# Last layer of a fused attention, mixture and feed-forward kernel: reordering scalar work, preparation steps and row gathers around the block products

## The chip, the cores and the metric

The kernel runs on 1 core of one Trainium2 chip. The metric is the device time of one execution in microseconds (us). Engines are named PE (matrix products), DVE (vector), ACT (scalar), POOL (GpSimd) and SP (which issues most DMAs); each works through its own queue of instructions in program order. L1286 means line 1286 of the kernel before.

## The reference, cut to what matters

An attention with pooled keys and values feeds a top-2 mixture of 8 experts; its 4608 rows of 512 numbers feed the last layer, the only part that the change touches:

```python
def _moe2_ref(x, w_in, w_out):      # x: 4608 x 512, w_in: 512 x 2048, w_out: 2048 x 512
    h = x @ w_in
    g = h * np.cos(h)
    return (g @ w_out).astype(np.float32)
```

The rows of x are sums of two gated expert outputs, which lie in an HBM buffer `yb` in the experts' order and have to be gathered row by row.

## The kernel before

All products are made from pairs of 16-bit numbers, high and low part, with three matmuls for each product. The order of each engine's work is the order of the program; the kernel schedules by hand.

**Chunks and quarters.** The last layer is a loop over 9 chunks of 512 rows (`c`, 0 to 8), and in each over 4 quarters (`q_`) of the 2048 columns of h. A quarter makes four blocks of h (b = 0 to 3) by seven block products in Strassen's manner (`prod`, L1215, 12 matmuls of 256 columns each), in the order 1, 2, 6, 7, 5, 3, 4. Three PSUM tiles carry them: `pb` takes products 1, 6, 5, 3 in turn, each added to what is there, `pa` takes 2, `pc` takes 7 and then 4. Between the products stand the matmuls of the quarter before that multiply g with w_out (`down`, L1245; `some(n)` issues n groups of three).

**What ties PE to the other engines.** After product 1, 6 and 5 ACT copies `pb` into scratch (L1274, L1286, L1294), and the next product into `pb` has to wait for that copy. DVE adds `pa` or `pc` to the copies (L1282, L1295, L1303); product 4 has to wait until L1295 has read `pc`. 

**The activation of a block.** `act_a` takes two DVE operations (L1222, L1223: the reduction of the angle) and two ACT operations (L1224 sine, L1225 square). `act_b`, issued later, takes one DVE operation (L1233), one ACT operation (L1234, the high part of g) and one on POOL (L1235, the low part). Block 2's `act_b` is issued in the next quarter, behind L1274.

**Preparation of the next chunk.** While chunk c runs, steps made by `prepare(c + 1)` fetch and convert the next chunk's rows: `gather` (two indirect DMAs from POOL, L1024, into one of four `yg` buffers), `comb1a` (ACT, L1033, writes the single `x2` tile), `comb1b` (DVE, L1039 and L1040), `comb2a` and `comb2b` (the scale: small DVE operations and one transposition on PE, L110), `sub` (DVE, L1079), `opa` (ACT, L1087) and `opb` (DVE, L1091, then a DMA transposition from SP). `opa` writes one of two `x2h` buffers, or spare room of the current `ht` tile. The four row blocks of a chunk have i = 0 to 3; the seven operands of the products have o = 0 to 6. There are nine steps, two slots for them in a quarter: slot A behind L1274 and block 2's `act_b`, ahead of L1282, and slot B behind product 7 and block 0's `act_b`, ahead of L1294. Step 9 (`opa` and `opb` of operand 6) is left for the next chunk's first quarter.

Of the kernel before, what the change touches and what calls it, by code (L numbers as in the profile page):

```python
# [12 lines left out]
AF = mybir.ActivationFunctionType  # L13
# [21 lines left out]
def tile_attn_moe_ffn(ctx: ExitStack, tc: tile.TileContext, q, k, v, wgate, wnoise, noise,  # L35
                      w1, w2, win, wout, out):
    nc = tc.nc
    V, A, PL, PE, SP = nc.vector, nc.scalar, nc.gpsimd, nc.tensor, nc.sync
# [580 lines left out]
    for u in range(NU):  # L619
        g, r, n = UNITS[u]  # L620
# [106 lines left out]
    def psum(nm, bufs):  # L727
        return pp_.tile([128, 512], F32, name=nm, bufs=bufs)
# [288 lines left out]
    NCF = len(CHF)  # L1017
    X2, GT, CB = {}, {}, {}

    def gather(c, i):  # L1020
        g, r = CHF[c][i]
        yg = wp.tile([128, 2, 512], F32, name="yg", bufs=4)
        for kk in range(2):
            PL.indirect_dma_start(out=yg[:, kk, :], out_offset=None, in_=yb[0:512 * E * (c + 1), :] if c < 2 else yb[:, :],  # L1024
                                  in_offset=bass.IndirectOffsetOnAxis(ap=yidx[:, g, kk, r:r + 1], axis=0))
        CB["yg", c, i] = yg
# [77 lines left out]
    def prepare(c, room):  # L1104


        def many(*x):
            return lambda: [f(c, *a) for f, *a in x]

        return [many((gather, 0), (gather, 1)),  # L1110
                many((gather, 2), (gather, 3), (comb1a, 0), (comb1a, 1)),
                many((comb1b, 0), (comb1b, 1), (comb1a, 2), (comb1a, 3)),
                many((comb1b, 2), (comb1b, 3), (comb2a,)),
                many((comb2b,), (opa, 0), (opa, 1), (opa, 2, room)),
                many((opb, 0), (opb, 1), (opb, 2), (sub, 3)),
                many((sub, 4), (sub, 5), (opa, 3), (opa, 4), (opa, 5, room)),
                many((opb, 3), (opb, 4), (opb, 5), (sub, 6)),
                many((opa, 6), (opb, 6))]

# [3 lines left out]
    for j in range(NJ + 1):  # L1123
        up = [(mm1, j, f) for f in range(8)] if j < NJ else []
        dn = []
        if j > 0:
            e, c = JOBS[j - 1]
# [76 lines left out]
    UB, DN, GQ = {}, {}, {}  # L1204
    PRODS = {1: (0, 0), 2: (1, 1), 3: (6, 2), 4: (2, 6), 5: (3, 3), 6: (4, 5), 7: (5, 4)}

    def prod(c, q_, n, ps, start):
        a_, b_ = PRODS[n]
        x = xt_tile(c, b_).rearrange("p (i s k) n -> p i s k n", i=2, s=2)
        for h in range(2):  # L1210
            f = 128 * (2 * q_ + h)
            o = ps[:, 256 * h:256 * h + 256].rearrange("p (i n) -> p i n", i=2)
            for k_ in range(2):
                for j, (sa, sb) in enumerate(((0, 0), (0, 1), (1, 0))):
                    PE.matmul(o, FW["in"][4 * a_ + 2 * sa + k_][:, f:f + 128], x[:, :, sb, k_, :],  # L1215
                              start=(start and h == 0 and k_ == 0 and j == 0), stop=(k_ == 1 and j == 2), skip_group_check=True)

    def act_a(c, q_, b, h):

        k4 = CB["k4", c]  # L1220
        y = wp.tile([128, 512], F32, name="ty", bufs=4)
        V.tensor_scalar(y, h, k4[:, 0:1], k4[:, 0:1], op0=OP.add, op1=OP.subtract)  # L1222
        V.tensor_sub(y, h, y)  # L1223
        A.activation(y, y, AF.Sin, scale=k4[:, 1:2])  # L1224
        A.activation(y, y, AF.Square, scale=math.sqrt(2.0 * CC))  # L1225
        UB[b] = (c, q_, h, y)

    def act_b(b):
        if b not in UB:
            return  # L1230
        c, q_, h, y = UB.pop(b)
        g = GQ[c, q_]
        V.scalar_tensor_tensor(y, y, CC, h, op0=OP.subtract, op1=OP.mult)  # L1233
        A.activation(g[:, 2 * b, :], y, AF.Copy)  # L1234
        PL.tensor_sub(g[:, 2 * b + 1, :], y, g[:, 2 * b, :])  # L1235

    def down(c, q_, b, tt, h):

        def f():
            t = 2 * (b % 2) + tt  # L1240
            if (c, t) not in DN:
                DN[c, t] = psum("ph", 4)
            ps, g, k_ = DN[c, t], GQ[c, q_], 8 * (b // 2) + 2 * q_ + h
            for i, (a_, b_) in enumerate(((0, 0), (0, 1), (1, 0))):
                PE.matmul(ps, g[:, 2 * b + a_, 256 * h + 128 * tt:256 * h + 128 * tt + 128], FW["out"][b_][:, k_, :],  # L1245
                          start=(q_ == 0 and b < 2 and h == 0 and i == 0), stop=(q_ == 3 and b > 1 and h == 1 and i == 2))
            if q_ == 3 and b > 1 and h == 1:
                g, r = CHF[c][t]
                o_ = wp.tile([128, 512], F32, name=("yt", "tm")[t % 2], bufs=2)
                A.activation(o_, ps, AF.Copy, scale=CB["k4", c][:, 2:3])  # L1250
                SP.dma_start(dap(out, (1152 * g + r) * 512, [[9 * 512, 128], [1, 512]]), o_)
        return f

    load_wout[1]()
    ds, st = [], []

    def some(n):
        for f in ds[:n]:
            f()
        del ds[:n]  # L1260

    def step():
        if st:
            st.pop(0)()

    for c in range(NCF):
        for q_ in range(4):
            if q_ == 0 and c + 1 < NCF:
                st += prepare(c + 1, lambda: g[:, 14:16, :])
            g = GQ[c, q_] = wp.tile([128, 16, 512], F16, name="ht", bufs=2)  # L1270
            cw = g[:, 8:16, :].rearrange("p a n -> p (a n)").bitcast(F32).rearrange("p (a n) -> p a n", n=512)
            pb, pa, pc = psum("py", 2), psum("pt", 2), psum("py", 2)
            prod(c, q_, 1, pb, True)
            A.activation(cw[:, 0], pb, AF.Copy)  # L1274
            act_b(2)
            if q_ == 0 and c and st:
                step()
            if q_ == 0 and c + 1 < NCF or q_:
                step()
            some(2)  # L1280
            prod(c, q_, 2, pa, True)
            V.tensor_add(cw[:, 0], pa, cw[:, 0])  # L1282
            act_a(c, q_, 0, cw[:, 0])
            some(2)
            prod(c, q_, 6, pb, False)
            A.activation(cw[:, 1], pb, AF.Copy)  # L1286
            some(2)
            prod(c, q_, 7, pc, True)
            act_b(0)
            if len(st) > 1 or q_ < 3:  # L1290
                step()
            some(1)
            prod(c, q_, 5, pb, False)
            A.activation(cw[:, 2], pb, AF.Copy)  # L1294
            V.tensor_add(cw[:, 2], pc, cw[:, 2])  # L1295
            act_a(c, q_, 3, cw[:, 2])
            some(2)
            prod(c, q_, 3, pb, False)
            act_a(c, q_, 1, pb)
            act_b(3)  # L1300
            some(1)
            prod(c, q_, 4, pc, False)
            V.tensor_add(cw[:, 1], pc, cw[:, 1])  # L1303
            act_b(1)
            act_a(c, q_, 2, cw[:, 1])
            some(16)
            ds += [down(c, q_, b, tt, h) for b in (0, 1, 3, 2) for tt in range(2) for h in range(2)]
    act_b(2)
# [29 lines left out]
```

## Time and profile before

| what | value |
|---|---|
| time, median of 3 runs | 1908.68 us (1900.23 to 1909.55) |
| profiled execution, own time | 1910.69 us |
| its span | 1908.9 us, 29354 instructions |
| PE busy over the span | 1737.7 us (91%) |
| DVE, ACT, POOL busy | 63%, 43%, 22% |
| last layer (first block product to the end) | from 1155.85 us on |

The page counts a matmul as busy from its issue to a modelled end, so neighbouring matmuls overlap. The rows below are read as: start, duration, engine, line, operation, tiles written and read, shape, count; in brackets how long the engine sat idle before it and for whom it waited. Times run from the start of the span.

### The profile page before, as it was taken

To read this page: it belongs to the slowest core of one execution; us is meant where nothing else is said; L and a number is where in the kernel's file an instruction comes from. 1 tells how busy PE (TensorE), PEld (TensorE's weight loads), DVE (VectorE), ACT (ScalarE), POOL (GpSimd) and SP (SyncE) were. 2 spreads that over 40 slices of the span, in tenths; PEclk is the share of its full clock that TensorE was granted. 3 is DMA by queue.
4 is the path that set the end of the run, shared out by engine and by line. 5 is a ranking of instruction groups with operands and counts; after the bars stand their busy time and mean duration, and the time that the engine had idled before them with its cause. 6 is when DMAs were issued, how large, how long until landed. Compare 5 with 4: busy or idle time off the path is not lost.

```text
span 1908.9 us, 29354 instructions
## 1 busy us (share of the span) xinstructions
PE 1737.7 (91%) x11657; PEld 1024.6 (54%) x11657; DVE 1203.0 (63%) x2190; ACT 825.2 (43%) x1602; POOL 420.3 (22%) x456
## 2 busy tenths in 40 slices
PE   5877755599999999999999997999999999999999
PEld 3555433246444644464445544666666666666665
DVE  6786465463657466535775143877878787787864
ACT  3655434133233333232333233555555555555554
POOL 1225534100000000000110012243242323424221
PEclk7988867699999999999999998999999999999999
DMA  9977323447553654555653543122231312213100
GB/s 264 314 242 288 133 78 144 122 162 206 141 182 97 192 159 151 194 139 157 185 177 86 210 138 116 34 73 57 66 75 32 88 34 72 74 49 89 34 29 23
DMA packets 233212, 243.56 MB, mean 128 GB/s; under 512 B 154352, under 2 KB 167664, under 8 KB 232432
## 3 DMA queue, kind: packets, MB, share of 16 engines
q1 hardware_dynamic: 210544, 183.97, 33.2%
q0 software_dynamic: 11520, 37.76, 6.0%
q10 hardware_dynamic: 11008, 19.93, 3.0%
q8 instruction: 92, 1.51, 0.3%
q14 instruction: 48, 0.39, 0.1%
HBM read 127.06 MB, written 78.12 MB: 107 GB/s over the span
## 4 chain that ended last, share of the span: by engine, by line
PE 43%; DVE 20%; ACT 11%; issue 4%; DMA 2%; ACTq 0%; DVEq 0%; POOL 0%; POOLq 0%; SPq 0%
PE ph L795 19%; PE py L820 18%; DVE ty L1223 5%; ACT ty L1224 5%; DVE ty L1222 4%; ACT ty L1225 4%; PE ph L1245 2%; DVE ty L1233 2%; PE py L1215 2%; DMA yg<-yb,yidx 2%; DVE ht L1091 1%; DVE ht L1282 1%; DVE x2h L1091 1%; PE py L835 1%; DVE x L1039 1%
## 5 line engine op out<-in xcount | busy, mean ns | idle before, releaser
L795 PE MATMUL ph<-xt,w 128*128 128x512 f16 (+1 forms) x2304 | 410.4, 336 | 9.6 <-DMA xt<-xs 9.6
L1245 PE MATMUL ph<-w,ht 128*128 128x512 f16 x1728 | 413.2, 379 | 0.0
L820 PE MATMUL py<-w,ht 128*128 128x512 f16 x1728 | 384.4, 379 | 0.2 <-DVE ht L808 0.2
L795 PEld LDWEIGHTS <-w 128*128 128x128 f16 x2304 | 214.8, 98 | 196.0 <-issue 14.6
L1235 POOL TENSOR_TENSOR ht<-ty,ht 128x512 f16<-128x512 f32 x144 | 181.4, 1271 | 469.6 <-ACT ht L1234 393.0
L808 DVE SCALAR_TENSOR_TENSOR ht<-ph,ht 128x512 f16<-128x512 f32 (+2 forms) x192 | 110.0, 574 | 269.3 <-ACT ht L807 269.2
L820 PEld LDWEIGHTS <-ht 128*128 128x128 f16 x1728 | 168.8, 98 | 199.0 <-DVE ht L808 0.7
L1245 PEld LDWEIGHTS <-ht 128*128 128x128 f16 x1728 | 169.2, 98 | 151.9 <-issue 0.3
L1215 PEld LDWEIGHTS <-st 128*128 128x128 f16 x1872 | 184.0, 98 | 93.1 <-issue 45.5
L1224 ACT ACTIVATE ty<-ty,k 128x512 f32<-128x512 f32 x144 | 103.9, 722 | 262.4 <-DVE ty L1223 248.1
L807 ACT ACTIVATE ht<-ph 128x512 f16<-128x512 f32 (+2 forms) x192 | 96.2, 502 | 182.5 <-PE ph L795 156.5
L1215 PE MATMUL py<-xt,st 128*128 128x256 f16 x1040 | 142.4, 276 | 23.7 <-ACT ht L1294 12.0
L823 ACT ACTIVATE yt<-py,ysc 128x512 f32<-128x512 f32 x72 | 49.3, 685 | 231.6 <-PE py L820 231.6
L1233 DVE SCALAR_TENSOR_TENSOR ty<-ty,ht 128x512 f32<-128x512 f32 x108 | 74.8, 692 | 110.8 <-ACT ty L1225 108.9
L1215 PEld LDWEIGHTS <-w 128*128 128x128 f16 x1152 | 113.2, 98 | 36.8 <-issue 1.0
L1215 PE MATMUL py<-w,st 128*128 128x256 f16 x832 | 111.7, 272 | 9.9 <-ACT ht L1286 6.4
L435 PE MATMUL xp<-vbd,et 128*64 128x144 f32 (+3 forms) x864 | 91.2, 354 | 22.1 <-issue 5.9
L1024 POOL DMA_INDIRECT yg<-yb,yidx x72 | 73.5, 1020 | 162.7 <-DMA yb<-yt 93.5
L1223 DVE TENSOR_TENSOR ty<-ht,ty 128x512 f32<-128x512 f32 x108 | 105.0, 972 | 3.7
L886 POOL TENSOR_TENSOR tm<-yg 128x512 f32<-128x512 f32 x32 | 34.4, 1076 | 302.2 <-DVE x L896 151.1
L1234 ACT ACTIVATE ht<-ty 128x512 f16<-128x512 f32 x144 | 90.1, 626 | 24.6 <-DVE ty L1233 24.6
L1222 DVE TENSOR_SCALAR ty<-ht,k 128x512 f32<-128x512 f32 x108 | 91.1, 844 | 8.0 <-DVE ht L1282 0.5
(240 smaller groups left out, 2084.5 us busy)
## 6 DMA issues: line engine op xcount, KB each, us to landing
yb<-yt ACTq DMA_DIRECT2D x72, 256.0 KB
st<-in_moe_w_dram SPq DMA_DIRECT2D x8, 2048.0 KB
yg<-in_moe_w_in_dram SPq DMA_DIRECT2D x32, 512.0 KB
yg<-in_moe_w_out_dram SPq DMA_DIRECT2D x32, 512.0 KB
yb<-zt SPq DMA_DIRECT2D x18, 768.0 KB
st<-in_moe_w_dram SPq DMA_DIRECT2D x8, 1536.0 KB
w<-in_k_dram SPq DMA_DIRECT2D x16, 512.0 KB
w<-in_v_dram SPq DMA_DIRECT2D x16, 512.0 KB
```

What stands on the lines that cost most here:

```text
L435: PE.matmul(xp[64 * b:64 * b + 64, c0:c0 + n], lhs[:, 64 * b:64 * b + 64], rhs, start=(c == cs[0][0]), stop=(c == cs[-1][0]), skip_group_c ...
L795: PE.matmul(ps[:, 0:n], w[:, a_, k_, 128 * f:128 * f + 128], xt[:, 4 * b_ + k_, 0:n], start=(i == 0), stop=(i == 11))
L807: A.activation(t[:, 0], p, AF.Relu)
L808: V.scalar_tensor_tensor(t[:, 1], p, 0.0, t[:, 0], op0=OP.max, op1=OP.subtract)
L820: PE.matmul(ps[0:m], ht[:, a_, f, 128 * t:128 * t + m], w[:, b_, f, :], start=(i == 0), stop=(i == 23))
L1215: PE.matmul(o, FW["in"][4 * a_ + 2 * sa + k_][:, f:f + 128], x[:, :, sb, k_, :], start=(start and h == 0 and k_ == 0 and j == 0), stop=(k_ ...
L1222: V.tensor_scalar(y, h, k4[:, 0:1], k4[:, 0:1], op0=OP.add, op1=OP.subtract)
L1223: V.tensor_sub(y, h, y)
L1224: A.activation(y, y, AF.Sin, scale=k4[:, 1:2])
L1233: V.scalar_tensor_tensor(y, y, CC, h, op0=OP.subtract, op1=OP.mult)
L1235: PL.tensor_sub(g[:, 2 * b + 1, :], y, g[:, 2 * b, :])
L1245: PE.matmul(ps, g[:, 2 * b + a_, 256 * h + 128 * tt:256 * h + 128 * tt + 128], FW["out"][b_][:, k_, :], start=(q_ == 0 and b < 2 and h == ...
```

## The change

It has three parts. (1) `act_a` is cut in two: the DVE pair stays, the ACT pair (sine, square) becomes `act_s`, and for block 0 it is issued behind the copy L1286; for blocks 3, 1 and 2 it directly follows `act_a` as before. (2) Slot A moves from ahead of L1282 to behind block 0's `act_a`; what is left of the last chunk's steps (`own`) goes just ahead of it. (3) The gathers of a chunk move out of its own steps into the steps of the chunk before (quarters 2 and 3); a list of eight steps of its own serves chunk 1.

```diff
+        def rows(c, *i):
+            return [(lambda c_, i=i: gather(c, i), i) for i in i] if c < NCF else []
+        if c == 1:
+            return [many(*rows(1, 0, 1)),
+                    many(*rows(1, 2, 3)),
+                    many((comb1a, 0), (comb1a, 1)),
+                    many((comb1b, 0), (comb1b, 1), (comb1a, 2), (comb1a, 3)),
+                    many((comb1b, 2), (comb1b, 3), (comb2a,)),
+                    many((comb2b,), (opa, 0), (opa, 1), (opa, 2, room)),
+                    many((opb, 0), (opb, 1), (opb, 2), (sub, 3), (sub, 4), (sub, 5), (opa, 3), (opa, 4), (opa, 5, room),
+                         *rows(2, 0, 1)),
+                    many((opb, 3), (opb, 4), (opb, 5), (sub, 6), (opa, 6), (opb, 6), *rows(2, 2, 3))]
-        return [many((gather, 0), (gather, 1)),
-                many((gather, 2), (gather, 3), (comb1a, 0), (comb1a, 1)),
+        return [many((comb1a, 0), (comb1a, 1)),
                 many((comb1b, 0), (comb1b, 1), (comb1a, 2), (comb1a, 3)),
                 many((comb1b, 2), (comb1b, 3), (comb2a,)),
-                many((comb2b,), (opa, 0), (opa, 1), (opa, 2, room)),
+                many((comb2b,)),
+                many((opa, 0), (opa, 1), (opa, 2, room), *rows(c + 1, 0, 1)),
                 many((opb, 0), (opb, 1), (opb, 2), (sub, 3)),
-                many((sub, 4), (sub, 5), (opa, 3), (opa, 4), (opa, 5, room)),
+                many((sub, 4), (sub, 5), (opa, 3), (opa, 4), (opa, 5, room), *rows(c + 1, 2, 3)),
                 many((opb, 3), (opb, 4), (opb, 5), (sub, 6)),
                 many((opa, 6), (opb, 6))]
...
-        A.activation(y, y, AF.Sin, scale=k4[:, 1:2])
+        UB[b] = (c, q_, h, y)
+
+    def act_s(b):
+        c, _, _, y = UB[b]
+        A.activation(y, y, AF.Sin, scale=CB["k4", c][:, 1:2])
         A.activation(y, y, AF.Square, scale=math.sqrt(2.0 * CC))
-        UB[b] = (c, q_, h, y)
...
-            if q_ == 0 and c + 1 < NCF:
-                st += prepare(c + 1, lambda: g[:, 14:16, :])
+            if q_ == 0:
+                own, st = st, prepare(c + 1, lambda: g[:, 14:16, :]) if c + 1 < NCF else []
...
             act_b(2)
-            if q_ == 0 and c and st:
-                step()
-            if q_ == 0 and c + 1 < NCF or q_:
-                step()
             some(2)
             prod(c, q_, 2, pa, True)
             V.tensor_add(cw[:, 0], pa, cw[:, 0])
             act_a(c, q_, 0, cw[:, 0])
+            while own:
+                own.pop(0)()
+            step()
             some(2)
             prod(c, q_, 6, pb, False)
             A.activation(cw[:, 1], pb, AF.Copy)
+            act_s(0)
             some(2)
             prod(c, q_, 7, pc, True)
             act_b(0)
-            if len(st) > 1 or q_ < 3:
+            if c == 0 or len(st) > 1:
                 step()
...
             act_a(c, q_, 3, cw[:, 2])
+            act_s(3)
...
             act_a(c, q_, 1, pb)
+            act_s(1)
...
             act_a(c, q_, 2, cw[:, 1])
+            act_s(2)
```

## Rows read from the trace of the kernel before

**Rows 1.** Waits of PE in the last layer: us in total, times, longest.

```profile
PE py L1215 <- ACT ht L1286: 17.7, 25, 3.0
PE py L1215 <- ACT ht L1294: 15.3, 8, 8.5
```

**Rows 2.** Timeline of PE, chunk 0, quarter 3: product 1, product 4, next quarter.

```profile
1222.51 1.47 PE L1215 MATMUL py<-xt,w 128*128 128x256 f16 x12
...
1236.84 0.38 PE L1215 MATMUL py<-xt,w 128*128 128x256 f16 x2
...
1242.04 1.47 PE L1215 MATMUL py<-w,w 128*128 128x256 f16 x12
```

**Rows 3.** Timeline of PE, chunk 4: product 1, product 3; product 1 of the next two quarters.

```profile
1570.56 1.47 PE L1215 MATMUL py<-w,w 128*128 128x256 f16 x12
...
1585.07 1.47 PE L1215 MATMUL py<-w,st 128*128 128x256 f16 x12 [0.68 <-ACT ht L1294]
...
1592.22 1.47 PE L1215 MATMUL py<-w,w 128*128 128x256 f16 x12
...
1612.46 1.47 PE L1215 MATMUL py<-w,w 128*128 128x256 f16 x12
```

**Rows 4.** Timeline of PE, chunk 5: product 1 of quarters 2 and 3, then chunk 6.

```profile
1693.79 1.47 PE L1215 MATMUL py<-xt,w 128*128 128x256 f16 x12
...
1713.80 1.47 PE L1215 MATMUL py<-xt,w 128*128 128x256 f16 x12
...
1733.56 1.47 PE L1215 MATMUL py<-w,w 128*128 128x256 f16 x12
```

**Rows 5.** Timeline of ACT, chunk 4, quarter 0: sine, two copies, `comb1a`.

```profile
1579.71 0.72 ACT L1224 ACTIVATE ty<-ty,k 128x512 f32<-128x512 f32 x1 [3.25 <-DVE ty L1223]
...
1581.00 0.58 ACT L1286 ACTIVATE ht<-py 128x512 f32<-128x512 f32 x1
...
1582.39 0.71 ACT L1033 ACTIVATE x<-yg,gates 128x512 f32<-128x512 f32 x1
...
1584.44 0.58 ACT L1294 ACTIVATE ht<-py 128x512 f32<-128x512 f32 x1
```

**Rows 6.** Timeline of DVE, chunk 4, quarter 0 (three rows) and quarter 1 (two).

```profile
1574.49 0.69 DVE L1233 SCALAR_TENSOR_TENSOR ty<-ty,ht 128x512 f32<-128x512 f32 x1 [1.51 <-ACT ty L1225]
1576.49 1.13 DVE L1091 SCALAR_TENSOR_TENSOR x2h<-x,xt4s,x2h 128x512 f16<-128x512 f32 x1 [1.31 <-ACT x2h L1087]
...
1578.92 0.69 DVE L1223 TENSOR_TENSOR ty<-ht,ty 128x512 f32<-128x512 f32 x1
...
1602.81 0.74 DVE L1039 SCALAR_TENSOR_TENSOR x<-yg,gates,x 128x512 f32<-128x512 f32 x1
...
1606.34 0.23 DVE L104 COPY mbc<-xm 128x128 f32<-128x128 f32 x1
```

**Rows 7.** Timeline of DVE, chunk 5: block 2's second operation, then quarter 3.

```profile
1714.70 1.52 DVE L1223 TENSOR_TENSOR ty<-ht,ty 128x512 f32<-128x512 f32 x1
...
1723.30 0.69 DVE L1233 SCALAR_TENSOR_TENSOR ty<-ty,ht 128x512 f32<-128x512 f32 x1 [1.51 <-ACT ty L1225]
...
1727.41 0.68 DVE L1295 TENSOR_TENSOR ht<-py,ht 128x512 f32<-128x512 f32 x1
```

**Rows 8.** Timeline of POOL, same stretch: low parts of blocks 3 and 1.

```profile
1713.23 2.45 POOL L1235 TENSOR_TENSOR ht<-ty,ht 128x512 f16<-128x512 f32 x2 [6.65 <-ACT ht L1234]
```

**Rows 9.** Timeline of all engines, chunk 0, quarter 0 and the start of quarter 1.

```profile
1162.91 0.63 ACT L1234 ACTIVATE ht<-ty 128x512 f16<-128x512 f32 x1 [0.27 <-DVE ty L1233]
...
1172.70 2.72 PE L1215 MATMUL py<-xt,st 128*128 128x256 f16 x12 [8.54 <-ACT ht L1294]
...
1175.08 0.95 POOL L1024 DMA_INDIRECT yg<-yb,yidx  x1 [0.30 <-issue]
...
1178.64 1.47 PE L1215 MATMUL py<-xt,w 128*128 128x256 f16 x12 [0.78 <-DVE ht L1303]
```

**Rows 10.** Engine busy time by window; last columns: granted PE clock, DMA share, GB/s.

```profile
1160.00:1180.00 20.00, 9.23 (x61) 6.82 (x59) 7.53 (x12) 8.24 (x13) 9.85 (x10) 0.74 0.53 172
```

More of the change, by code (lines that the diff above doesn't have):

```diff
@@ L1264, in step @@
             st.pop(0)()
+    own = []
     for c in range(NCF):
         for q_ in range(4):
-            if q_ == 0 and c + 1 < NCF:
-                st += prepare(c + 1, lambda: g[:, 14:16, :])
+            if q_ == 0:
+                own, st = st, prepare(c + 1, lambda: g[:, 14:16, :]) if c + 1 < NCF else []
             g = GQ[c, q_] = wp.tile([128, 16, 512], F16, name="ht", bufs=2)
```

## The prediction

> **What bounds the kernel now.** I read the page first: the last layer is the stretch where PE is nearly always busy, and the change touches only that. Then the waits of PE there: almost all of its idle time is two waits, for the copy L1286 (25 times) and for the copy L1294 (8 times, once per chunk that prepares another), 33.0 us together [rows 1]. That is the prize. Then the timelines, quarter by quarter. A quarter without any wait takes 1242.04 - 1222.51 = 19.53 us [rows 2]; this is the floor, set by PE's own matmuls, and product 4 starts 14.33 into it. A common chunk loses against it: quarter 0 1592.22 - 1570.56 = 21.66, loss 2.13; quarter 1 20.24, loss 0.71 [rows 3]; quarter 2 20.01, loss 0.48 (of which 0.1 is the scale's transposition, which stays); quarter 3 19.76, loss 0.23 [rows 4]. Sum 3.55 us. The reader is to see that three of four quarters are already close to the floor, that quarter 0 holds most, and that each loss is an ACT or DVE instruction being late by less than a microsecond or two. So the question is where each late instruction stands after the change.
>
> **The sine pair behind L1286.** In quarter 0 L1286 starts only when the pair has ended: sine at 1579.71, L1286 at 1581.00 [rows 5], though its product had ended long before. Behind the change L1286 no longer waits for this pair, but slot A's ACT work now stands directly ahead of L1286, and slot A's DVE work stands behind L1223 of block 0.
>
> **Quarter 0, chunks 2 to 7.** Slot A now holds the left-over `opa`/`opb` of operand 6 and two `comb1a`. `comb1a` writes the single `x2` tile that `opb` still reads, so ACT waits for `opb`, which waits behind L1282, L1222 and L1223. In chunk 4's times: block 2's L1233 ends at 1575.18; from the end of `opb` (1577.62) to the end of L1223 (1579.61) the three operations take 2.0 [rows 6], so they now end at 1577.2. `opb` costs at most its 1.13: 1578.3. Two `comb1a` of about 0.7 [rows 5]: L1286 at 1579.7, 1.3 sooner than 1581.00, and product 5 is no longer late. But then the pair follows: L1286 0.55, from the sine to where slot B's `comb1a` starts 1582.39 - 1579.71 = 2.68, two `comb1a` 1.4: L1294 at 1584.3, against 1584.44 [rows 5]. Product 3 waits for it as before, and the wait, once split between two copies, now stands in one place. Loss 2.1 (bounds 1.8 to 2.8), where it was 2.13. The gather's landing no longer delays `comb1a`, but in the earlier chain that was worth only 0.7, which L1286 ahead of the pair takes back.
>
> **Quarter 1.** `comb1b` 2, 3 and `comb2a` now stand in slot A and `comb2b` in slot B of the same quarter. From the first of these L1039 to the end of the copy L104 it is 1606.57 - 1602.81 = 3.76 [rows 6]. They start when L1223 of block 0 ends, about 6.2 into the quarter (product 2 starts 2.6 in, 1.6 more to L1282, 2.0 for the three operations), so the copy is there at 9.9; PE reaches the transposition behind product 7 at about 9.5 and now waits 0.3 to 0.5, plus some 0.15 for each restart. A wait for L1274 of 0.2 to 0.7 comes on top, since quarter 0 hands on its lateness with three output copies in ACT's queue. Loss 1.2 (0.8 to 1.8), where it was 0.71.
>
> **Quarter 2.** Three `opa` on ACT fit ahead of L1286, the two gathers lie on POOL ahead of block 0's L1235, which nobody needs before the next quarter. Loss 0, where it was 0.48.
>
> **Quarter 3.** The third `opa` needs `sub` 5, which now comes behind L1223 of block 0: L1286 at 8.1 to 8.9 into the quarter, still in time for product 5. But the pair follows it, so L1233 of block 0 comes at 10.1 to 10.8; before it came at 1723.30 - 1713.80 = 9.50 and three `opb` and a `sub` put L1295 at 13.61, ending 14.3 [rows 4, 7]: just in time for product 4 (14.33 [rows 2]). Now L1295 ends at 14.9 to 15.7 and product 4 is late. Loss 0.8 (0.3 to 1.6), where it was 0.23.
>
> Sum of a common chunk: 2.1 + 1.2 + 0 + 0.8 = 4.1 (2.9 to 6.2) against 3.55. Six chunks: +3.3 us (-3.9 to +15.9).
>
> **DVE beside POOL.** L1223 takes 1.52 when POOL's L1235 runs beside it (1713.23 for 2.45), and 0.69 alone [rows 6 to 8]. Block 2's L1235 will now run while L1222 and L1223 of block 0 do, in quarters 0 and 3 above all, where up to now an `opb` or a `sub` lay beside it. That is up to 0.83 for each of these quarters, and it is what the upper bounds above hold; I take about a third: by the sums above L1222 and the low part become ready almost together, and where DVE comes first nothing in these rows says that it is slowed. The Trainium skill (SBUF — State Buffer, section "SBUF: two separate sides") says that the pair of ports which DVE and GpSimd share is locked for a whole instruction, and that the loser blocks. These rows agree with that; by the rule in its full force (0.55 more in two quarters of six chunks) the sum of six chunks would stand near +10 instead of +3.3.
>
> **Chunk 0.** In quarter 0 ACT waited for the first gathers, and with it L1294 and product 3 (8.54 idle, to 1172.70). After the change nothing stands between L1234 of block 0 (1162.91) and L1294: product 3 at 1164.1, 8.6 sooner. Its 12 matmuls ran in 2.72 instead of 1.47, at a granted clock of 0.74 over the stretch after that idle time [rows 9, 10]; at full clock quarter 1 starts some 1.0 sooner still: gain 9.6. Against that, POOL's gathers end no sooner (1176.03), and both low parts of blocks 3 and 1 (2.45 [rows 8]) stand behind them: 1178.5. PE, 9.6 earlier, wants block 1's low part at 1176.3 and waits 2.3. Quarters 1 and 2 lasted 1222.51 - 1178.64 = 43.87, 4.8 over the floor [rows 2, 9]; I count 2.3 there, 0.4 for block 0's low part, and 1.6 for `comb2b` followed at once by three `opa` ahead of L1294: 4.4 in all. Quarter 3 had no loss; now its slot A holds three `opb`, three `sub` and three `opa` in sequence and slot B three `opb`, a `sub`, `opa` 6, `opb` 6. L1286 comes behind the third `opa`, at 11.7, where product 5, due some 9.8 into the quarter, wants it begun by 9.1: 2.5; L1294 behind `opa` 6, which waits for `sub` 6 behind three `opb`: 4.1. With restarts 6.9. Chunk 0: 9.6 + 0.4 - 6.9 = 3.1 gained, less what a lowered clock after these waits costs: 0 to 6 (1.25 for each 12 matmuls at the lower level [rows 9]), taken as 2.5. So -0.6 (-3.1 to +3).
>
> **Chunks 1 and 8.** Chunk 1 has no left-over, so quarter 0's 2.13 go: -1.5 with the other quarters' changes. Chunk 8 has nothing to prepare: its wait for L1286 goes, 2.13 less the 0.84 for L1294: -1.3.
>
> **Sum:** +3.3 - 0.6 - 1.5 - 1.3 = -0.1 us. The profiled execution took 1910.69 (span 1908.9 and 1.8 around it), 2.0 above the median of the runs shown. So I predict 1910, the same within what can be told (0.5% of the time, 9.5 us).
>
> **Rivals.**
> 1. *The waits go and none comes back (faster).* If `comb1a` waits less for `opb`, L1295 in quarter 3 stays under 14.3 and the transposition finds its copy, seven preparing chunks win up to 3.4 each, 24 us, with chunk 8 and chunk 0's 3.1: 1882. For it: L1286 really leaves the pair's shadow, 17.7 us of waiting [rows 1], and DVE has slack behind L1223. Against it: the single `x2` tile, and a DVE queue that ended only just in time [rows 7]. If half of that comes true, 1896. Chance 0.25, between 1880 and 1900.
> 2. *The slowed pair and the long steps decide (slower).* L1223 of block 0 takes 1.52 in quarters 0 and 3, each chunk loses the upper 6.2: +15.9, chunk 0 +3, less 2.8: 1926. It decides from about 0.7 more in each of both quarters (six times 1.4 and 3.3 make over 9.5). For it: [rows 7, 8]; against it: it needs the low part to start first nearly every time. Chance 0.20, between 1920 and 1930.
> 3. *The change does not do what it says.* L1286 stays late because the steps' ACT work stands ahead of it, and the wait merely moves to L1294 and L1295. This is the forecast; 0.55, own range 1900 to 1919.
>
> **How the numbers follow.** The likeliest case is 3: 1910. Leaving out the far half of rival 1 and the far half of rival 2 (0.2 together) gives 1892 to 1923. Faster 0.25, same 0.55, slower 0.20.
>
> **What would show each step.** In the new trace: waits of PE for L1286 gone in chunks 1 to 8; waits for L1294 in quarter 0 of chunks 2 to 7 of about 2 us each; a wait of PE's L110 for L104; product 4 waiting for L1295 in quarter 3; in chunk 0 product 3 at 1164, a `down` group waiting for L1235 near 1178, and some 7 us of waits in quarter 3. The prediction is wrong if quarter 0 of the common chunks drops under 20.5 us (then rival 1) or quarter 3 rises over 21 (then rival 2).

## The result, and the profile after

The changed kernel takes 1927.88 us (median of 4 runs, 1925.05 to 1930.07); the kernel before takes 1909.12 beside it. The ratio on record is 1.0113, 95% interval 1.0086 to 1.014: 1.1% slower, above the predicted range of 1892 to 1923. (The ratios here and below are those on record; the quotient of the two medians can differ by some tenths of a per cent, 1.0098 here.) The profiled execution took 1926.75, with a span of 1925.0.

One warning before the spans are read. The last layer starts at 1155.85 in the profile of before and at 1147.69 in that of after; over the profiles of this study it lies between 1146.5 and 1162.8, though no kernel differs in the work ahead of it. So the measure used below is the *layer*: from the start of the first block product to the end of the span. Before it lasts 1908.90 - 1155.85 = 753.05, after 1925.0 - 1147.69 = 777.3: 24.3 longer.

Line numbers move: the block products L1215 are now L1228; L1286, L1294 and L1295 (copy of product 5, copy and sum of product 3 and 4) are L1302, L1311 and L1312; L1282 is L1295; L1274, the copy of product 1, is L1291; L1222, L1223 are L1235, L1236; L1233, L1234, L1235 are L1249, L1250, L1251; the output copy is L1266. L104, L110, L1024, L1033, L1039, L1087, L1091, L1092 keep theirs.

The waits of PE in the last layer, which answer to [rows 1] (us in total, times, longest):

```profile
PE pt L110 <- DVE mbc L104: 13.6, 8, 1.9
PE py L1228 <- ACT ht L1311: 13.1, 9, 1.7
PE py L1228 <- ACT ht L1302: 11.4, 7, 9.1
PE py L1228 <- DVE ht L1312: 5.4, 7, 0.8
PE ph L1261 <- POOL ht L1251: 2.9, 2, 2.1
```

The old first line, 25 waits for the copy of product 5, has shrunk to 7, and one of these alone is 9.1. In its place stands the scale's transposition L110, which waits in each of the eight preparing chunks for the copy L104.

One label of the rows of before has to be set right first. Counted from 1155.85, chunk 5 starts at 1570.56, chunk 6 at 1652.22 and chunk 7 at 1733.56, so what [rows 3, 5, 6] and the prediction call chunk 4 is chunk 5, and what [rows 4, 7, 8] call chunk 5 is chunk 6. The differences read from them stay the same.

The same by quarter, PE in chunk 5, answering to [rows 3, 4] (product 1 of quarter 0; product 5; product 3; product 1 of quarter 1; product 6; the transposition; product 4 of quarter 3):

```profile
1576.74 1.47 PE L1228 MATMUL py<-w,w 128*128 128x256 f16 x12
...
1587.07 1.47 PE L1228 MATMUL py<-w,st 128*128 128x256 f16 x12 [0.39 <-ACT ht L1302]
...
1591.43 1.47 PE L1228 MATMUL py<-w,st 128*128 128x256 f16 x12 [1.60 <-ACT ht L1311]
...
1598.58 1.47 PE L1228 MATMUL py<-w,w 128*128 128x256 f16 x12
...
1604.48 1.47 PE L1228 MATMUL py<-w,st 128*128 128x256 f16 x12 [0.19 <-ACT ht L1291]
...
1610.46 0.33 PE L110 MATMUL pt<-idf,mbc 128*128 128x128 f32 x1 [1.90 <-DVE mbc L104]
...
1656.14 0.38 PE L1228 MATMUL py<-w,w 128*128 128x256 f16 x2 [0.83 <-DVE ht L1312]
```

Quarter 0 lasts 1598.58 - 1576.74 = 21.84, a loss of 2.31 against the floor of 19.53; the four quarters of this chunk last 21.84, 22.45, 19.53 and 20.78. The transposition is where the prediction's wait of 0.3 to 0.5 became 1.90. Product 4 of quarter 3 waits for the sum that reads its PSUM tile, L1312.

The clock joins in. Windows of after: the layer, the stretch around the end of chunk 0's long wait, the stretch around the transposition's wait in chunk 3, and two microseconds behind that wait (busy time and instructions of PE, PEld, DVE, ACT, POOL; granted clock; DMA share; GB/s):

```profile
1147.69:1925.00 777.31, 721.97 (x4761) 468.46 (x4759) 558.91 (x780) 412.21 (x665) 241.02 (x208) 0.98 0.23 57
1215.50:1225.70 10.20, 2.69 (x13) 1.87 (x13) 1.44 (x3) 4.41 (x7) 0.00 (x0) 0.60 0.75 112
1436.00:1441.00 5.00, 3.09 (x18) 1.92 (x17) 4.29 (x15) 1.34 (x3) 1.12 (x1) 0.83 0.00 0
1440.00:1442.00 2.00, 2.00 (x12) 1.38 (x10) 0.49 (x4) 0.00 (x0) 1.03 (x1) 0.50 0.00 0
```

Behind the wait the granted clock is 0.50, which is 1.2 of 2.4 GHz. This happens in four of the seven preparing chunks behind chunk 0 (1, 3, 4 and 6). In chunks 3, 4 and 6 quarter 1 then lasts 24.13 instead of 22.45: 1.68 more each. Chunk 1's lasts 23.48 with such a fall; there is no chunk 1 without one to set beside it.

By chunk the layer changed by +3.0 us (chunk 0), +2.4 (1), +2.6, +3.7, +2.6, +2.9, +4.9, +3.3 (2 to 7) and -1.3 (8).

### The profile page after: what moved, and what is told of

It is laid out like the page before. It is cut to its first block, busy times and chain, and to the rows that moved or that the text cites. A ratio compares the mean times of both kernels' runs of the same rounds, so it can differ in the third digit from the quotient of the medians.

```text
span 1925.0 us, 29347 instructions
## 1 busy us (share of the span) xinstructions
PE 1743.1 (91%) x11657; PEld 1027.6 (53%) x11657; DVE 1216.8 (63%) x2190; ACT 824.5 (43%) x1602; POOL 413.7 (21%) x456
## 4 chain that ended last, share of the span: by engine, by line
PE 58%; DVE 13%; ACT 7%; issue 2%; DMA 1%; POOL 1%; ACTq 0%; DVEq 0%; SPq 0%; POOLq 0%
PE ph L795 19%; PE py L820 18%; PE ph L1261 11%; PE py L1228 8%; DVE ty L1235 3%; DVE ty L1236 2%; ACT ty L1241 2%; PE pt L1228 2%; ACT ty L1242 1%; DVE x L1039 1%; DVE xam L1040 1%; PE py L835 1%; DVE x2h L1091 1%; DVE ht L1295 1%; DVE ht L1091 1%
## 5 line engine op out<-in xcount | busy, mean ns | idle before, releaser
L1251 POOL TENSOR_TENSOR ht<-ty,ht 128x512 f16<-128x512 f32 x144 | 176.7, 1238 | 499.8 <-ACT ht L1250 453.7
L1228 PEld LDWEIGHTS <-st 128*128 128x128 f16 x1872 | 185.7, 99 | 85.4 <-issue 35.7
L1228 PE MATMUL py<-xt,st 128*128 128x256 f16 x1040 | 143.0, 278 | 19.4 <-ACT ht L1302 10.3
L1249 DVE SCALAR_TENSOR_TENSOR ty<-ty,ht 128x512 f32<-128x512 f32 x108 | 76.3, 706 | 130.2 <-ACT ty L1242 99.8
L1228 PEld LDWEIGHTS <-w 128*128 128x128 f16 x1152 | 112.7, 98 | 44.2 <-issue 9.6
L1228 PE MATMUL py<-w,st 128*128 128x256 f16 x832 | 114.1, 277 | 6.8 <-ACT ht L1311 4.8
L1250 ACT ACTIVATE ht<-ty 128x512 f16<-128x512 f32 x144 | 90.1, 626 | 55.6 <-DVE ty L1249 53.1
L1235 DVE TENSOR_SCALAR ty<-ht,k 128x512 f32<-128x512 f32 x108 | 107.1, 992 | 8.0 <-DVE ht L1312 0.5
L1024 POOL DMA_INDIRECT yg<-yb,yidx x72 | 72.0, 1000 | 162.8 <-DMA yb<-yt 93.5
L1236 DVE TENSOR_TENSOR ty<-ht,ty 128x512 f32<-128x512 f32 x108 | 104.0, 963 | 3.7
```

## The experiments

**Theory A**: the change costs time at four places, each with its cause. Quarter 1's transposition waits because the combination steps now follow product 2's sum; quarter 0 and quarter 3 lose to operand 6 and the subtractions in one slot; chunk 0's quarter 3 loses to data transposed while the gathers run. The rivals are named with each run: that the sine pair's new place does it, that the gathers do it, or that DVE is slow beside POOL.

The change has three parts, in the order of its description: (1) the sine pair behind the next copy, (2) new slots and step lists, (3) gathers sooner. The first runs take before and add parts; the rest mend after.

**Part 1 alone**, on before, for block 0, whose pair stood ahead of the copy:

```diff
-        A.activation(y, y, AF.Sin, scale=k4[:, 1:2])
-        A.activation(y, y, AF.Square, scale=math.sqrt(2.0 * CC))
         UB[b] = (c, q_, h, y)
+        if b:
+            act_s(b)
...
             A.activation(cw[:, 1], pb, AF.Copy)
+            act_s(0)
```

> The kernel before with part 1 of the change alone: block 0's sine and square behind the copy L1286, slots and gathers as before. Theory A (the copy is freed, but the DVE chain that starts the pair is where it was, so L1294 in quarter 0 and L1295 in quarters 1 to 3 come at the same times): the waits for L1286 fall from 17.7 to under 4, those for L1294 and L1295 rise, and the time falls by 2 to 6 us. Theory B (the waits for L1286 were a loss of their own): the time falls by 14 to 20 us.

1910.04 against 1914.99, ratio 0.9993 (0.997 to 1.0016); layer 753.4, 0.3 more than before. The first two waits of PE in its last layer (L1300 and L1301 here are L1294 and L1295 of before):

```profile
PE py L1215 <- ACT ht L1300: 28.1, 9, 10.1
PE py L1215 <- DVE ht L1301: 3.0, 6, 1.0
```

The waits for product 5's copy are gone and those for product 3's have grown from 15.3 to 28.1: 17.7 + 15.3 = 33.0 before [rows 1], 31.1 now. The wait moves one copy further, as the prediction said. The fall of 2 to 6 us that was expected is not seen, though the interval (0.3% down to 0.2% up) does not exclude it. The trace shows what stood against it: the granted clock falls to 0.50 in quarter 0 of chunks 4, 5 and 7, at single waits of 3.17, 2.10 and 2.29, and these quarters last 25.68, 23.46 and 23.65, where the other four of chunks 1 to 7, with waits of 1.86 to 2.42 and no fall, last 21.55 to 22.11. Before, where the wait is split between two copies, has no such fall behind chunk 0.

**Part 3 alone**, on before: the gathers of chunk c + 2 are issued while chunk c + 1 is prepared.

```diff
-        return [many((gather, 0), (gather, 1)),
-                many((gather, 2), (gather, 3), (comb1a, 0), (comb1a, 1)),
+        return [many(*(rows(1, 0, 1) if first else [])),
+                many(*(rows(1, 2, 3) if first else []), (comb1a, 0), (comb1a, 1)),
...
-                many((comb2b,), (opa, 0), (opa, 1), (opa, 2, room)),
+                many((comb2b,), (opa, 0), (opa, 1), (opa, 2, room), *rows(c + 1, 0, 1)),
...
-                many((sub, 4), (sub, 5), (opa, 3), (opa, 4), (opa, 5, room)),
+                many((sub, 4), (sub, 5), (opa, 3), (opa, 4), (opa, 5, room), *rows(c + 1, 2, 3)),
```

> The kernel before with part 3 alone: gathers of chunk c+2 in quarters 2 and 3 of chunk c, slots and activation as before (chunk 1's gathers stay in chunk 0). Theory A (only the landing waits inside L1294's wait go, 0.4 to 2.4 us in each of seven chunks): the time falls by 4 to 9 us, chunk 0 stays as it was, and nothing gets slower in quarters 2 and 3. Theory B (gathers beside the operands' transpositions and ahead of POOL's low parts cost there what they save): within 3 us of the kernel before.

1894.69, ratio 0.992 (0.989 to 0.9949); layer 742.3. The common chunk lasts 80.2 (19.97, 20.14, 20.11, 19.99): quarter 0 lost 2.13 and now 0.44. The early gathers are worth 10.7 us of the layer, more than the 4 to 9 expected, where the prediction gave their landing 0.7 a chunk. Chunk 0 did not stay as it was: it takes 87.59 instead of 86.19.

**Parts 1 and 3**, the two edits together:

> The kernel before with parts 1 and 3: the pair behind L1286 and the early gathers, the slots where they were. With the gathers alone a common chunk took 80.2 us and its waits were all for L1286, 0.4 to 0.6 in each quarter. Theory A (freeing L1286 shifts these waits to L1294 and L1295, as with the pair alone): a common chunk 79.5 to 80.2, the layer within 6 us of that with the gathers alone. Theory B (those waits were a loss of their own): a common chunk 78.3 to 78.8, the layer 10 to 13 us shorter.

1894.74, ratio 0.9915 (0.9887 to 0.9944); layer 741.0. The first two waits of PE:

```profile
PE py L1219 <- ACT ht L1304: 18.2, 9, 10.1
PE py L1219 <- DVE ht L1305: 6.7, 15, 1.0
```

So with the gathers early, moving the pair costs nothing, and the two parts together gain. What remains of the change, part 2, costs 777.3 - 741.0 = 36 us of the layer on top of them. That is a net figure: part 2 also shortens chunk 0's quarter 0 from 22.42 to 13.01, and lengthens its quarter 3 from 20.38 to 32.92. The next runs divide the loss.

**`comb2b` later in quarter 1**, on after, so that PE's transposition stands ahead of product 4 and not behind product 7:

```diff
-            if c == 0 or len(st) > 1:
+            if (c == 0 or len(st) > 1) and not (c and q_ == 1):
                 step()
...
             act_b(3)
             some(1)
+            if c and q_ == 1:
+                step()
             prod(c, q_, 4, pc, False)
```

> The changed kernel, but in chunks 1 to 7 the step with comb2b (the scale's transposition on PE) is issued ahead of product 4 of quarter 1 instead of ahead of product 5. Theory A (most of the loss is PE waiting in quarter 1 for the copy L104, 1.9 us a chunk, and the lowered clock behind four of these waits): the waits for L104 in chunks 1 to 7 go from 13.4 us to under 1, quarter 1 of these chunks takes 20.0 to 20.9 instead of 22.4 to 24.1, the clock stays up there, and the time falls by 15 to 21 us. Theory B (the slot behind the first chain makes DVE late, and PE pays for it at whatever waits next): the wait comes back at products 3 and 4 of the same quarter and the time falls by less than 6 us.

1919.82, ratio to before 1.0031 (1.0002 to 1.006); layer 759.4, 17.9 less than after. Quarter 1 lasts 20.89, and in no chunk does the clock fall there; quarters 0 and 3 stay at 21.84 and 20.78. The waits for L104 are gone, and only 0.40 a chunk comes back, at product 3 of the same quarter. This place cost 17.9 us of the layer, the falls of the clock included.

**The output copies ahead of the last sine pair**, on after. ACT's queue then no longer ends the quarter with that pair in front of the output copies:

```diff
-            act_s(2)
             some(16)
+            act_s(2)
```

> The changed kernel with one line moved: block 2's sine and square are issued behind the last group of w_out matmuls and their output copies, so that the three output copies run while ACT waits for DVE, and product 1's copy comes 1.7 us sooner in quarter 1. Theory A (the prediction's price of the wait for L104 failed because L1282 has to wait for that copy): the wait for L104 falls from 1.9 to 0.3 to 0.7, quarter 1 of chunks 2 to 7 from 22.4 to 24.1 down to 20.6 to 21.2, no clock drop there, 12 to 18 us less in the layer. Theory B (the price failed because comb1b and the DVE pair are slowed beside POOL): the wait stays over 1.4.

One timed execution: 1922.99; layer 762.5, 14.8 less than after. Quarter 1 lasts 21.10, and the clock stays up there. Chunk 5, quarter 1: the first operation of block 0's DVE pair, block 2's low part on POOL, and the transposition:

```profile
1605.59 1.47 DVE L1235 TENSOR_SCALAR ty<-ht,k 128x512 f32<-128x512 f32 x1
1605.62 1.16 POOL L1251 TENSOR_TENSOR ht<-ty,ht 128x512 f16<-128x512 f32 x1 [3.50 <-ACT ht L1250]
...
1611.06 0.33 PE L110 MATMUL pt<-idf,mbc 128*128 128x128 f32 x1 [1.25 <-DVE mbc L104]
```

The wait went from 1.90 to 1.25, not to the 0.3 to 0.7 expected. One thing stands out: L1235 of block 0 takes 1.47 here, beside POOL's subtraction for block 2. Is that the rest of the wait, or only its neighbour?

**The same without POOL's subtraction for block 2**, on top of the run before this: zeros are written in place of that low part, so its share of the product with `w_out` is left out.

```diff
-        PL.tensor_sub(g[:, 2 * b + 1, :], y, g[:, 2 * b, :])
+        if b == 2:
+            PL.memset(g[:, 2 * b + 1, :], 0.0)
+        else:
+            PL.tensor_sub(g[:, 2 * b + 1, :], y, g[:, 2 * b, :])
```

> The changed kernel with the output copies ahead of block 2's sine (as in the run before), and POOL fills block 2's low part with zeros, which waits for no activation, instead of subtracting: the low part of one block in four is left out of the product with w_out. What is left of quarter 1's wait for L104 is 1.25 us. Theory A (the first DVE operation of block 0, L1235 of this kernel, is slowed by POOL's subtraction beside it): L1235 in quarter 1 takes 0.55 to 0.6 instead of 1.47, the wait for L104 falls to 0.2 to 0.5, quarter 1 of chunks 2 to 7 from 21.1 to 20.1 to 20.5. Theory B (it is slow because it follows the addition that writes its input): L1235 stays at 1.2 to 1.5 and the quarter at 21.1.

One timed execution: 1890.41 (before on the same chip: 1902.6); layer 742.1. In chunk 5 the sum of quarter 1 and the operation behind it:

```profile
1579.00 0.68 DVE L1298 TENSOR_TENSOR ht<-pt,ht 128x512 f32<-128x512 f32 x1
1579.79 0.55 DVE L1235 TENSOR_SCALAR ty<-ht,k 128x512 f32<-128x512 f32 x1
```

The operation is back at 0.55; the waits for L104 fall from 9.6 (8 times) to 2.1; quarter 1 goes from 21.10 to 20.12, quarter 0 from 21.85 to 20.87, quarter 3 from 20.78 to 20.3. The slowing is worth about 1.0, 1.0 and 0.5 in these quarters. The trace of after has a test of its own: in quarter 3 of chunk 3 alone L1235 takes 0.55 instead of 1.17, and this quarter lasts 20.15 instead of 20.78. Not all of the 20 us by which the layer is shorter than in the run above are the slowing's: chunk 0's quarter 3 falls from 32.50 to 29.09, since POOL, with nothing to wait for, issues the gathers there 4 to 5 us sooner in the quarter, ahead of the transposition.

**Chunk 2's gathers behind chunk 0's quarter 3**, on after. Only these four gathers (two DMAs each) move:

```diff
-                    many((opb, 0), (opb, 1), (opb, 2), (sub, 3), (sub, 4), (sub, 5), (opa, 3), (opa, 4), (opa, 5, room),
-                         *rows(2, 0, 1)),
-                    many((opb, 3), (opb, 4), (opb, 5), (sub, 6), (opa, 6), (opb, 6), *rows(2, 2, 3))]
+                    many((opb, 0), (opb, 1), (opb, 2), (sub, 3), (sub, 4), (sub, 5), (opa, 3), (opa, 4), (opa, 5, room)),
+                    many((opb, 3), (opb, 4), (opb, 5), (sub, 6), (opa, 6), (opb, 6))]
...
+            if c == 0 and q_ == 3:
+                for i in range(4):
+                    gather(2, i)
```

> The changed kernel, but chunk 2's eight gathers are issued at the end of chunk 0's quarter 3 instead of in its two steps. Theory A (the operands' DMA transpositions land late in that quarter because the gathers' rows lie beside them on the same DMA engines): the wait for L1302 there falls from 9.1 to 2.5 to 4 us, the quarter from 32.9 to 24 to 27 us, and a new wait of ACT for the gathers comes in chunk 1's quarter 0, 3 to 8 us. Theory B (two buffers and one step that fills, empties and fills them again cost that much by themselves): the wait stays at 8 to 9 us.

One timed execution: 1927.47; layer 772.6, 4.7 less than after; chunk 0's quarter 3 falls from 32.92 to 28.81. After, timeline of all engines in that quarter (the first and last gather DMA of one step, the transposition between them, the operand that waits, products 5 and 3):

```profile
1209.64 0.98 POOL L1024 DMA_INDIRECT yg<-yb,yidx  x1
...
1211.23 2.88 SPq L1092 DMA_TRANSPOSE w<-x2h  x2
...
1214.22 1.14 POOL L1024 DMA_INDIRECT yg<-yb,yidx  x1 [0.30 <-issue]
...
1217.90 0.72 ACT L1087 ACTIVATE x2h<-x,xt4s 128x512 f16<-128x512 f32 x1 [9.64 <-DMA w<-x2h]
...
1223.01 2.72 PE L1228 MATMUL py<-xt,st 128*128 128x256 f16 x12 [9.10 <-ACT ht L1302]
...
1229.74 1.47 PE L1228 MATMUL py<-xt,st 128*128 128x256 f16 x12 [1.69 <-ACT ht L1311]
```

And the transposition, the operand and product 5 with the gathers moved:

```profile
1216.66 2.58 SPq L1092 DMA_TRANSPOSE w<-x2h  x2
...
1219.54 0.72 ACT L1087 ACTIVATE x2h<-x,xt4s 128x512 f16<-128x512 f32 x1 [5.84 <-DMA w<-x2h]
...
1222.71 2.72 PE L1227 MATMUL py<-xt,st 128*128 128x256 f16 x12 [3.37 <-ACT ht L1301]
```

From the transposition's issue to the operand that waits for its source buffer: 1217.90 - 1211.23 = 6.7 us beside the gathers, 1219.54 - 1216.66 = 2.9 without. The wait for the copy falls from 9.10 to 3.37. The quarter wins 4.1, less than that and less than the 6 to 9 expected: its next wait, for product 3's copy, grows from 1.69 to 2.38, and the 12 matmuls behind that one now run at the lower clock too (2.72 instead of 1.47). The price came where it was expected, but smaller: in chunk 1's quarter 0 ACT waits 0.50 and 2.03 for the gathers, and the quarter lasts 21.06 instead of 19.53.

**Operand 6 and the subtractions early**, on top of the later `comb2b`: operand 6 is prepared at the end of quarter 3, not in the next chunk's slot A, and subtractions 4 and 5 go ahead of quarter 3's first chain.

```diff
+            if q_ == 3 and 0 < c < NCF - 1:
+                sub(c + 1, 4)
+                sub(c + 1, 5)
...
+            six = q_ == 3 and 0 < c < NCF - 1
+            if six:
+                opa(c + 1, 6)
             act_s(2)
+            if six:
+                opb(c + 1, 6)
             some(16)
```

> The kernel with the late transposition (first experiment), and two more edits: operand 6 of the next chunk is prepared at the end of quarter 3 (opa ahead of block 2's sine, opb behind its DVE pair) and not in the next chunk's slot A, and sub 4 and 5 go ahead of the first chain of quarter 3, where they stood before the change. Theory A (quarter 0 is late because comb1a waits for opb 6 behind the first chain; quarter 3 because the third opa waits for sub 5 behind it): quarter 0 of chunks 2 to 7 takes 19.5 to 20.2 instead of 21.84, quarter 3 of chunks 1 to 7 19.6 to 20.1 instead of 20.78, the time falls by 15 to 20 us against the first experiment. Theory B (POOL's low part beside the first chain is what makes both late: L1222 took 1.2 to 1.5 there instead of 0.55): quarter 0 stays over 21, quarter 3 over 20.4.

1886.65, ratio to before 0.9879 (0.9849 to 0.9908); layer 732.3, 27.1 less than with `comb2b` alone. Chunks 1 to 7 last 78.83 each, chunk 4 0.1 more (19.53, 20.24, 19.53, 19.53): quarters 0 and 3 stand on the floor, and the gain is more than the 15 to 20 expected. Theory B is not simply refuted by that, since in most of these quarters block 0's first DVE operation (L1234 here) is no longer slowed either (0.55 to 0.60). But in quarter 0 of chunk 4 it still takes 1.47, and this quarter lasts 19.53 too: with operand 6 out of the way the slowing costs nothing.

**All of it together**: the later `comb2b`, operand 6 and the subtractions early, the output copies ahead of the last pair, and chunk 0's steps and gathers spread over its quarters. The core of what is new moves chunk 0's operands 0 to 2 to the end of quarter 2, operand 5 to the end of quarter 3:

```diff
-                    many((comb2b,), (opa, 0), (opa, 1), (opa, 2, room)),
-                    many((opb, 0), (opb, 1), (opb, 2), (sub, 3), (sub, 4), (sub, 5), (opa, 3), (opa, 4), (opa, 5, room),
-                         *rows(2, 0, 1)),
-                    many((opb, 3), (opb, 4), (opb, 5), (sub, 6), (opa, 6), (opb, 6), *rows(2, 2, 3))]
+                    many((comb2b,)),
+                    many((opb, 2), (sub, 3), (sub, 4), (sub, 5), *rows(2, 0, 1)),
+                    many((opa, 3), (opb, 3), (opa, 4), (opb, 4), (sub, 6))]
...
+            if c == 0 and q_ == 2:
+                opa(1, 0)
+                opa(1, 1)
+                opa(1, 2, room)
+            if c == 0 and q_ == 3:
+                opa(1, 5, room)
...
+            some(16)
             act_s(2)
-            some(16)
```

> All together: early gathers, pair behind L1286, slot A behind the first chain, late transposition, operand 6 at the end of quarter 3, sub 4 and 5 behind block 2's pair in quarter 2, the output copies ahead of block 2's sine, and chunk 0's steps spread so that no buffer is filled twice in a step. If the accounting by quarters holds, quarters take 19.5 to 19.9, chunk 0 73 to 77 us, the layer 715 to 728 us where it took 753 before: 25 to 38 us faster than the kernel before. If PE's waits only move (the rival all along), the layer stays over 738.

1870.88 (1868.83 to 1872.45), ratio to before 0.9792 (0.9741 to 0.9843): faster than both kernels, and 1.6 to 2.6% faster than before. The layer lasts 718.9, as expected; chunk 0 75.48, chunk 1 81.2, chunks 2 to 7 78.2 to 78.35. The largest three waits of PE left in the layer, of which the last falls in chunk 1's quarter 0 (22.37 instead of 19.53) and is again one for a transposition by DMA:

```profile
PE py L1226 <- ACT ht L1309: 2.2, 2, 1.5
PE py L1226 <- DVE ht L1322: 2.0, 1, 2.0
PE py L1226 <- DMA w<-ht: 1.8, 1, 1.8
```

## Why the prediction was wrong

It called the places rightly and two sizes wrongly: quarter 1 of the preparing chunks, and chunk 0's quarter 3. The forecast for the layer was -0.1 (six common chunks +3.3, chunk 0 -0.6, chunk 1 -1.5, chunk 8 -1.3); the traces show +24.3 (+20.0, +3.0, +2.4, -1.3). The medians show +18.8, less than the layer's sum, because of the scatter of the layer's start.

The signs that the prediction named for being wrong did not show: quarter 0 stayed over 20.5 (21.84) and quarter 3 under 21 (20.78). They watched the two quarters whose size was about right, and none watched quarter 1.

**What held.** *Quarter 0*: forecast loss 2.1, measured 2.31. The chain of ACT and DVE is the one that the prediction drew: `comb1a` behind `opb` 6, product 5's copy behind it, and the pair and two more `comb1a` ahead of product 3's. That the size came so near is partly luck. The pair L1235 and L1236 ended 7.77 into the quarter instead of 6.6, since L1235 took 1.47 instead of 0.55; `opb` (0.75 instead of at most 1.13) and the four `comb1a` (1.33 and 1.32 for two instead of 1.4, and the next copy starts before they end) were priced too high, and together they gave most of it back. Product 5 is still late, by 0.39 in each of these chunks. *Quarter 2*: forecast 0, measured 0 (19.53). *Quarter 3*: product 4 waits for L1312, loss 1.25 against 0.8 (0.3 to 1.6), and 0.62 in chunk 3. *Chunk 8*: -1.3, as forecast. *Chunk 0's quarter 0*: forecast gain 9.6, measured 22.79 - 13.01 = 9.78 (22.79 is 1178.64 [rows 9] - 1155.85); the down group's wait for block 1's low part is 2.1 against 2.3. Its quarters 1 and 2 lose 4.2 against 4.4 (the three terms given there make 4.3). *The gathers in quarter 2* cost nothing. *Moving the pair*: nothing gained or lost in the time, as the run of part 1 shows.

**The step that failed: quarter 1.** The forecast was that "the copy is there at 9.9", hence a wait of 0.3 to 0.5 and a loss of 1.2; the copy ended at 11.8, the wait was 1.90 and the loss 2.92. The sum took the start of the chain from product 2 alone ("product 2 starts 2.6 in, 1.6 more to L1282"). But that sum reads the copy of product 1 too. In quarters 2 and 3, where no output copies stand ahead of that copy, the sum starts 4.2 into the quarter, just as the forecast has it; in quarter 1 it does not. After, ACT in chunk 5 around the start of quarter 1 (product 1 started at 1598.58):

```profile
1600.83 0.72 ACT L1241 ACTIVATE ty<-ty,k 128x512 f32<-128x512 f32 x1 [2.08 <-DVE ty L1236]
1601.58 0.63 ACT L1242 ACTIVATE ty<-ty 128x512 f32<-128x512 f32 x1
1602.12 0.67 ACT L1266 ACTIVATE tm<-ph,k 128x512 f32<-128x512 f32 x1
1602.69 0.68 ACT L1266 ACTIVATE yt<-ph,k 128x512 f32<-128x512 f32 x1
1603.26 0.69 ACT L1266 ACTIVATE tm<-ph,k 128x512 f32<-128x512 f32 x1
1603.83 0.60 ACT L1291 ACTIVATE ht<-py 128x512 f32<-128x512 f32 x1
```

Block 2's pair, then three output copies, then the copy. DVE and POOL from there:

```profile
1604.46 0.69 DVE L1295 TENSOR_TENSOR ht<-pt,ht 128x512 f32<-128x512 f32 x1 [1.52 <-ACT ht L1291]
1605.26 1.20 DVE L1235 TENSOR_SCALAR ty<-ht,k 128x512 f32<-128x512 f32 x1
1606.49 0.69 DVE L1236 TENSOR_TENSOR ty<-ht,ty 128x512 f32<-128x512 f32 x1
1607.11 0.74 DVE L1039 SCALAR_TENSOR_TENSOR x<-yg,gates,x 128x512 f32<-128x512 f32 x1
...
1610.17 0.23 DVE L104 COPY mbc<-xm 128x128 f32<-128x128 f32 x1
```

```profile
1605.03 1.15 POOL L1251 TENSOR_TENSOR ht<-ty,ht 128x512 f16<-128x512 f32 x1 [4.84 <-ACT ht L1250]
```

The sum starts 1604.46 - 1598.58 = 5.88 into the quarter instead of 4.2: 1.7 late, and its idle time ahead ends on the copy. L1235 takes 1.20 beside the low part, against 0.55 in the run without block 2's subtraction: 0.65, and the prediction's three operations of 2.0 had no room for it. The combination itself took 3.29 where 3.76 was counted: -0.5. Together the copy ends 1.9 later than forecast. The prediction did see the three output copies; it priced them as 0.2 to 0.7 of PE's own wait for the copy (0.19 here) and left them out of DVE's chain. The run with the copies ahead of the pair shows the first cause, the run without block 2's low part the second, and the run with `comb2b` later shows what the place is worth: 17.9 us of the layer.

**The clock behind it was not counted there.** The forecast had a price for it in chunk 0 only. Chunks 3, 4 and 6 pay 1.68 each (5.0 of the six chunks' 20.0), and chunk 1 has a fall as well. With the wait shortened, to 1.25 or to nothing, the clock did not fall there.

How the six chunks add up: quarter 1, 6 x (2.92 - 1.2) = 10.3, and 0.35 more in chunk 7; the clock 5.0; quarter 3, 5 x 0.45 less 0.2 in chunk 3 = 2.1; quarter 0, 6 x 0.21 = 1.3; and the chunks of before last 82.05 in the mean, 0.38 more than the 3.55 of loss over the floor that the sum was set against (chunk 4's quarter 0 alone took 23.38): -2.3. This makes the 16.7 between +3.3 and +20.0.

Chunk 1 was forecast at -1.5 and changed by +2.4. Its quarter 0 had only 1.45 to give, not the 2.13 that was taken over from a later chunk (20.98 - 19.53); quarter 2 gave 0.48, quarter 3 cost 1.02, and quarter 1, with its fall of the clock, 3.34.

**Chunk 0's quarter 3.** The forecast was 6.9, as 2.5 for L1302 and 4.1 for L1311 with restarts; and 2.5 for the clock. Measured: 32.92 - 19.53 = 13.4, with 9.10 and 1.69 of waits and 2.6 for the rest, the lowered clock among it (0.60 over 1215.50 to 1225.70; the 12 matmuls behind the wait took 2.72 instead of 1.47). The first term failed, 9.10 for 2.5; the second came out smaller, 1.69 for 4.1. The prediction counted only ACT's and DVE's work ahead of the copy. But the `opa` of operands 3 and 4 write the two `x2h` buffers, and each must first have been read by a transposition by DMA, of operand 0 and 1: the first `opa` waits to 1217.90 (9.64 idle), the next to 1221.14 (2.52 idle). That transposition ran beside the gathers that the same change had put there, and the first buffer came free after 6.7 instead of 2.9. It was a transfer that the prediction should have followed: it counted the gathers' issues on POOL, and not that their data share the DMA engines with it.

**The rivals.** Rival 2 was closest in time (1926) by another road: DVE's slowing beside POOL exists, and in quarters 0 and 3 together it has about the size that rival 2 gave it (1.0 and 0.5), but the larger losses are those above. Its place was partly wrong: the operation that is slowed is L1222 (here L1235, 1.47 and 1.17), while L1223 stays at 0.69, and quarter 1 pays 1.0 as well. Rival 1 did not come true for this change. What it hoped for needs another order of steps: with operand 6, the subtractions and `comb2b` elsewhere only 0.40 a chunk is left of the waits, 1886.65, and 1870.88 with chunk 0 mended.

**What stays open.** The loss from part 2 was removed in steps (17.9 or 14.8 for quarter 1, 27.1 more for quarters 0 and 3), and they make 45, more than the 36 that part 2 costs: they also remove waits that the kernel with parts 1 and 3 still has (its common chunk lasts some 80.2, the mended one 78.83). So they are no split of the 36. Why the clock fell behind four of seven waits of almost the same length was not tried. It is not the chunk alone: in the run with chunk 2's gathers moved the same waits of 1.90 stand in quarter 1 of chunks 1 to 7, and the clock falls in chunks 3 and 5.

## What to carry to other kernels

When a step is moved behind a sum, follow all inputs of that sum through their own queues, not the one that the matmul delivers: here it was the other operand, a copy behind three output copies on an engine with plenty of idle time. A wait that has been moved is priced only when the chain behind its new place has been followed to the next thing that PE needs, DMA transfers included, and transfers that are started sooner by the same change run beside those that something now waits for. And undo the parts one at a time: two of three here were worth 12 us of the layer together, and the third lost 36.

## What the runs showed that had not been expected

- The transposition by DMA and the gathers hold each other up. The DMA view of after from 1209 to 1222 (queue, kind: packets, MB, share of 16 engines) shows both at once:

```profile
q1 hardware_dynamic: 3168, 0.79, 50.9%
q0 software_dynamic: 320, 1.05, 38.8%
```

The same 3168 packets with the gathers moved, from 1214 to 1226:

```profile
q1 hardware_dynamic: 3168, 0.79, 29.1%
```

Their time is 0.509 x 13 = 6.6 us on all 16 engines beside 1.05 MB of gathers, and 0.291 x 12 = 3.5 without. The gathers pay as well. Their 320 packets take 0.388 x 13 = 5.0 us there, and 0.376 x 10 = 3.8 in the run without block 2's low part (1203 to 1213), where most of them go ahead of the transposition:

```profile
q0 software_dynamic: 320, 1.05, 37.6%
```

- A DVE operation on data in SBUF that meets POOL's subtraction ended 0.28 after it in both cases looked at: L1235 from 1605.26 to 1606.46 beside POOL's to 1606.18 above. It takes 0.55 alone, 1.20 there, and 1.47 in the run with the copies first, where it was recorded 0.03 ahead of POOL's. The Trainium skill (SBUF — State Buffer, section "SBUF: two separate sides") calls the pair of ports that the two engines share an exclusive lock, held for the whole instruction by whoever starts first. In the first case DVE comes second and waits, which agrees with that, though only 0.28 of its 0.55 lie behind POOL's end; in the second, DVE is the one that starts first by the record, if only by 0.03, and still is the one that waits.
- The mean of L1235's group over the layer's steady part falls from 1007 ns to 839 ns with block 2's subtraction gone (first row with it, second without):

```profile
L1235 DVE TENSOR_SCALAR ty<-ht,k 128x512 f32<-128x512 f32 x94 | 94.7, 1007 | 7.2 <-DVE ht L1312 0.5
```

```profile
L1235 DVE TENSOR_SCALAR ty<-ht,k 128x512 f32<-128x512 f32 x95 | 79.8, 839 | 7.2 <-DVE ht L1298 0.5
```

- The early gathers alone were worth 0.8% (ratio 0.992), in a kernel where no wait of PE names a gather. ACT's do: behind chunk 0 it waited for gathers 8 times, 6.9 us in all, and with the gathers early not once.
